# The last stage of a fused attention and spectral-mix kernel: part of an add moved to VectorE and GpSimd, identity matmuls issued earlier, and idle matmuls between the last spectral mixes

## The chip, the cores and the metric

One Trainium2 chip, one of its cores. The metric is the device time in microseconds of one execution of the whole program; a median over several executions is given. Five engines take part, each with its own instruction queue: TensorE (PE; its weight loads are listed as PEld), VectorE (DVE), ScalarE (ACT), GpSimd (POOL) and SyncE (SP). Transfers run on 16 DMA engines; here they are triggered from SP and from POOL.

## The reference

Linear attention over 8 batches, 8 heads, 576 rows and head size 64 gives x with 8 x 576 rows of 512 features. Then, per batch:

```python
X = rfft(x, axis=1)                       # along the 576 rows
Yr = einsum('bmd,mde->bme', Xr, w_r) - einsum('bmd,mde->bme', Xi, w_i)   # first 64 modes only
Yi = einsum('bmd,mde->bme', Xr, w_i) + einsum('bmd,mde->bme', Xi, w_r)
y = irfft(Y, n=576, axis=1)
u = x + y
out = u + maximum(u @ w_ch, 0)
```

The output is 8 x 576 x 512 in fp32, 9.44 MB. The mix weights w_r and w_i hold 64 matrices of 512 x 512 each and are read in fp32.

## The kernel before, in words

Batches are taken in four pairs (`bp`), features in four groups of 128 (`g`). The main loop (L503 to L571) walks 16 units of one group and one pair: feature maps, the attention sums, the forward transform by matmul with a table. In between stand the **mixes** (`mix`, L412 to L453): one takes 8 modes of w_r or w_i for one group, loaded by one DMA of 1 MB from POOL's queue, and adds 16 small matmuls into a PSUM bank, 8 for each call (two calls, `i` = 0 and 1, make one set `o` of 8 modes). Until L572 every engine is held to the written order (`InOrder`, L25); from L573 on a scheduler may reorder what the engines get, within the data's dependences.

After the units come the mixes of the last group. Each second call now ends a set of modes: VectorE adds the earlier groups' sum and stores it as `yst` (L437), SP sends `yst` to `yall` (which lies in the buffer XT, so the profile calls it XT), TensorE transposes `yst` by four identity matmuls, ScalarE copies the result to `yT` (L443), four matmuls multiply it by w_ch, ScalarE copies that to `zst` (L451), and SP sends `zst` to `zall` (L452). `yall` and `zall` thus hold the spectrum of y and of y @ w_ch. Between these mixes run the 36 `channels` calls (L460 to L471), which compute x @ w_ch for one **chunk** of 128 rows and leave it in `xw`. The calls are used up before the last four mix calls, so these have nothing between them.

The **last stage** (L599 to L626) makes the output, chunk by chunk: 36 chunks, nine for each pair, number `n` = 8 being the leftover rows of both batches. For each chunk two PSUM banks are filled: one with x (an identity matmul, L607) plus the inverse transform of `yall` (a matmul with the table CI, L609, or two half-width ones for `n` = 8, L613), the other with x @ w_ch (identity, L607) plus the inverse transform of `zall`. ScalarE takes the relu of the second into `rl` (L618), and VectorE adds the first and `rl` into the output tile `of` or `ofr` (L620). SP stores four chunks at a time, 1 MB (L622), and each pair's leftover in two halves (L626).

The PSUM pool of this stage, `pst`, has eight banks, and it is opened only after the two earlier pools `ps1` (four tiles of one bank) and `ps2` (two tiles of two banks) are closed (L594 to L596). `rl` has two buffers.

Of the kernel before, what the change touches and what calls it, by code (L numbers as in the profile page):

```python
# [10 lines left out]
F32 = mybir.dt.float32  # L11
BF16 = mybir.dt.bfloat16
I32 = mybir.dt.int32
ACT = mybir.ActivationFunctionType
ALU = mybir.AluOpType
# [4 lines left out]
DMODEL = 512  # L20
NG = 4
NP = 4
# [21 lines left out]
def kernel(  # L44
# [13 lines left out]
    nc = tc.nc  # L58
    pe, dve, act = (InOrder(tc, e) for e in (nc.tensor, nc.vector, nc.scalar))
# [9 lines left out]
    def one(shape, dt=F32):  # L69
        return ps1.tile(shape, dt, name="one", tag="one")  # L70

    def two(shape, dt=F32):
        return ps2.tile(shape, dt, name="two", tag="two")
# [6 lines left out]
    XTb = [pers.tile([128, 10, B_, NMODES], BF16, name=f"XT{i}") for i in range(2)]  # L80

    pw_cm = tc.tile_pool(name="pw", bufs=8)
    pw = pw_cm.__enter__()
# [223 lines left out]
    ident_b = const.tile([128, 128], BF16, name="ident_b")  # L307
# [26 lines left out]
    wchb = const.tile([128, 4, 512], BF16, name="wchb")  # L334
    CF = const.tile([128, 6, 4, 64], BF16, name="CF")
    CI = const.tile([128, 5, 128], BF16, name="CI")
# [8 lines left out]
    def sc(i):  # L345
# [4 lines left out]
        out=ang[:, :, 1, :],  # L350
        in0=sf.unsqueeze(2).to_broadcast([128, 5, 64]),
        in1=mf.unsqueeze(1).to_broadcast([128, 5, 64]),
        op=ALU.mult,
# [4 lines left out]
        out=rnd, in0=ang, scalar1=1.0 / S_, scalar2=MAGIC, op0=ALU.mult, op1=ALU.add)  # L358
    dve.tensor_scalar(
        out=rnd, in0=rnd, scalar1=-MAGIC, scalar2=-float(S_), op0=ALU.add, op1=ALU.mult)  # L360
# [48 lines left out]

    pys = {}  # L410

    def mix(g, w, wt, XT):  # L412

        o, i = w // 2, w % 2
        if i == 0:
            pys[o] = one([128, DMODEL])
        py = pys[o]
        for t in range(2):
            s0 = 2 - 2 * t + 4 * i
            for j in range(4):  # L420
                pe.matmul(
                    py[32 * j:32 * j + 32, :],
                    lhsT=XT[:, s0:s0 + 4, :, 32 * t + 4 * o + j].rearrange("p r b -> p (r b)"),
                    rhs=wt[:, 4 * t + j, :], start=(i == t == 0), stop=(i == t == 1),
                )
        if i == 0:
            return
        del pys[o]
        if g == 0:
            act.copy(yacc[:, o, :], py)  # L430
        elif g < NG - 1:
            dve.tensor_tensor(
                out=yacc[:, o, :], in0=py, in1=yacc[:, o, :], op=ALU.add)
        else:

            yst = pb.tile([128, DMODEL], BF16, name="yst")
            dve.tensor_tensor(out=yst, in0=py, in1=yacc[:, o, :], op=ALU.add)  # L437
            sp.dma_start(
                yall[16 * o:16 * o + 16], yst)
            pt = one([128, 4, 128], BF16)  # L440
            for dc in range(4):
                pe.transpose(pt[:, dc, :], yst[:, dc * 128:(dc + 1) * 128], ident_b)
            yT = pb.tile([128, 4, 128], BF16, name="yT")  # L443
            act.copy(yT, pt)
            pz = one([128, DMODEL])
            for dc in range(4):
                pe.matmul(
                    pz, lhsT=yT[:, dc, :], rhs=wchb[:, dc, :],
                    start=(dc == 0), stop=(dc == 3))
            zst = pb.tile([128, DMODEL], BF16, name="zst")  # L450
            act.copy(zst, pz)  # L451
            sp.dma_start(  # L452
                zall[16 * o:16 * o + 16], zst)  # L453

    def chunk(bp, n):
        if n < 8:
            return xs[:, :, bp, 2 * n:2 * n + 2, :].rearrange("p g h d -> p g (h d)")
        return xs[:, :, bp, 16:18, :].rearrange("p g h d -> p g (h d)")

    def channels(bp, n):  # L460
        x = chunk(bp, n)
        pt = one([128, 4, 128], BF16)
        for g in range(NG):
            nc.tensor.transpose(pt[:, g, :], x[:, g, :], ident_b)  # L464
        xT = pb.tile([128, 4, 128], BF16, name="xT")
        nc.vector.tensor_copy(xT, pt)  # L466
        pf = one([128, DMODEL])
        for g in range(NG):
            nc.tensor.matmul(  # L469
                pf, lhsT=xT[:, g, :], rhs=wchb[:, g, :], start=(g == 0), stop=(g == 3))  # L470
        nc.scalar.copy(xw[:, bp, n, :], pf)  # L471


    wts = {}
    wq = [(g, mg) for g in range(NG) for mg in range(2 * NO)]
    mixq = []

    def next_w(n):
        for _ in range(n):
            if wq:  # L480
                key = wq.pop(0)
                wts[key] = wload(*key)

    def some(n):
        for _ in range(n):
            if mixq:
                key = mixq.pop(0)
                mix(*key, wts.pop(key), XTb[key[0] % 2])
                if key == (0, 2):
                    clear(XTb[1])  # L490
                if key not in held:
                    next_w(1)
# [79 lines left out]
    for e in (pe, dve, act, pool, sp):  # L572
# [4 lines left out]
    pb_cm = tc.tile_pool(name="pb", bufs=2)  # L577
    pb = pb_cm.__enter__()
    xw = pb.tile([128, NP, 9, DMODEL], BF16, name="xw", bufs=1)
    zall = pb.tile([128, B_, DMODEL], BF16, name="zall", bufs=1)  # L580
    yall = XTb[0].rearrange("p s b m -> p (s b m)")[:, 0:B_ * DMODEL].rearrange(
        "p (b e) -> p b e", b=B_)
    todo = [(bp, n) for bp in range(NP) for n in range(9)]
    while mixq:
        key = mixq.pop(0)
        if key not in wts:
            next_w(1)
        mix(*key, wts.pop(key), XTb[key[0] % 2])
        next_w(1)
        for _ in range(2):  # L590
            if todo:
                channels(*todo.pop(0))

    ps1_cm.__exit__(None, None, None)  # L594
    ps2_cm.__exit__(None, None, None)
    pst = ctx.enter_context(tc.tile_pool(name="pst", bufs=8, space=bass.MemoryType.PSUM))  # L596


    for bp in range(NP):  # L599
        of = [pw.tile([128, 4, DMODEL], F32, name="of", tag="wt") for _ in range(2)]  # L600
        ofr = pb.tile([128, DMODEL], F32, name="ofr")
        for n in range(9):
            ps = []
            for base, src in ((chunk(bp, n), yall), (xw[:, bp, n, :], zall)):
                p = pst.tile([128, DMODEL], F32, name="pt", tag="pt")
                po = p.rearrange("p (g e) -> p g e", g=4) if src is yall else p
                nc.tensor.matmul(po, lhsT=ident_b, rhs=base, start=True, stop=False)  # L607
                if n < 8:
                    nc.tensor.matmul(p, lhsT=CI[:, n % 4, :], rhs=src[:, 2 * bp + n // 4, :],  # L609
                                     start=False, stop=True)  # L610
                else:
                    for i in range(2):
                        nc.tensor.matmul(  # L613
                            p[64 * i:64 * i + 64, :], lhsT=CI[:, 4, 0:64],
                            rhs=src[:, 2 * bp + i, :], start=False, stop=True)
                ps.append(p)
            rl = pb.tile([128, DMODEL], F32, name="rl")
            nc.scalar.activation(rl, ps[1], ACT.Relu)  # L618
            o = of[n // 4][:, n % 4, :] if n < 8 else ofr
            nc.vector.tensor_tensor(out=o, in0=ps[0], in1=rl, op=ALU.add)  # L620
            if n in (3, 7):
                nc.sync.dma_start(  # L622
                    out[2 * bp + n // 4, 0:512, :].rearrange("(p c) e -> p c e", c=4),
                    of[n // 4])
        for i in range(2):
            nc.sync.dma_start(out[2 * bp + i, 512:576, :], ofr[64 * i:64 * i + 64, :])  # L626
    pb_cm.__exit__(None, None, None)
    pw_cm.__exit__(None, None, None)

# [1 line left out]
_INS = ['q', 'k', 'v', 'w_phi', 'moe_w_r', 'moe_w_i', 'moe_w_ch']  # L631
# [26 lines left out]
```

The softmax here doesn't subtract the row's maximum and nothing guards it: scores larger than these inputs give would overflow.

## Time and profile before

| what | value |
|---|---|
| median of 7 executions | 482.41 us (480.55 to 482.71) |
| the profiled execution, its own time | 480.75 us |
| its span on the core | 478.9 us |
| TensorE matmul busy | 326.8 us (68%) |
| VectorE busy | 288.8 us (60%) |
| ScalarE busy | 256.4 us (54%) |
| GpSimd busy | 104.0 us (22%) |
| bytes written to HBM | 9.44 MB |
| mean granted TensorE clock | 0.882 |

The profiled execution lies 1.7 us below the median. Its span starts and ends with the core's work; the 1.8 us between span and time lie around it. In the rows below, a time without another word is in us from the start of the span. The profile page gives busy time by engine, the span cut into 40 slices, the chain of work that ended last, and groups of instructions with the mean time of one. The trace can also be asked for instructions in order of time, for busy time and granted clock in chosen stretches, and for all instructions that touch one tile.

### The profile page before, as it was taken

The page shows a single profiled execution, that of the slowest core. Times are in us where ns is not written, and L with a number is a line of the kernel's source. Part 1 is how long each engine was busy: PE and PEld are TensorE (multiplying, and loading weights), DVE is VectorE, ACT ScalarE, POOL GpSimd, SP SyncE. Part 2 cuts the span into 40 slices and gives each one's busy share as a digit, 9 for nine tenths or more (in the row PEclk, how much of TensorE's full clock was granted, in tenths as well). Part 3 has the DMA queues.
Part 4 walks back from the last instruction along what each step waited for, and adds up shares of the span by engine and source line. Part 5 has one row for each costly group of instructions (what it writes and reads, how often), then busy time and mean ns, then how long its engine had stood idle before and what let it go on. Part 6 is the DMA issues. An engine that isn't in the chain of part 4 may idle for free. (4 is left out here: it accounts for less than half of the span.)

```text
span 478.9 us, 8054 instructions
## 1 busy us (share of the span) xinstructions
PE 326.8 (68%) x3104; PEld 202.7 (42%) x3133; DVE 288.8 (60%) x524; ACT 256.4 (54%) x435; POOL 104.0 (22%) x139
## 2 busy tenths in 40 slices
PE   2563776787767876786587646747667676737994
PEld 1352554555544544554465334523333333312441
DVE  5678579779779778878869657632221222200874
ACT  3761767767776965865675727401232333301763
POOL 8332122124412331322043121131211110000000
PEclk9999977759999988977978859777999999985998
DMA  8999999999999999999999999999999999990676
GB/s 140 212 213 208 212 207 212 215 212 204 217 210 210 212 217 205 214 216 205 215 218 203 219 204 207 207 208 208 206 207 215 216 215 214 214 192 25 242 296 252
DMA packets 111318, 99.68 MB, mean 208 GB/s; under 512 B 16944, under 2 KB 109744, under 8 KB 110256
## 3 DMA queue, kind: packets, MB, share of 16 engines
q0 software_dynamic: 84496, 76.03, 97.5%
q1 hardware_dynamic: 26784, 23.14, 18.5%
q8 instruction: 24, 0.39, 0.3%
q14 instruction: 14, 0.11, 0.1%
HBM read 163.64 MB, written 9.44 MB: 361 GB/s over the span
## 5 line engine op out<-in xcount | busy, mean ns | idle before, releaser
L37 ACT ACTIVATE AB<-two 128x1024 bf16<-128x1024 f32 x64 | 62.0, 1021 | 46.8 <-DVE mk L37 46.4
L37 ACT ACTIVATE AQ<-two 128x1024 bf16<-128x1024 f32 x64 | 62.7, 1043 | 16.3 <-PE two L37 11.8
L471 ACT CAST xw<-one 128x512 bf16<-128x512 f32 x36 | 21.1, 585 | 67.6 <-PE one L469 60.3
L37 DVE TENSOR_TENSOR nd<-one,e 128x390 f32<-128x390 f32 x48 | 26.8, 558 | 49.6 <-PE one L37 49.5
L37 PE MATMUL one<-wt,XT 128*32 128x512 bf16 x472 | 38.5, 429 | 23.9 <-DMA wt<-in_moe_w_i_dram 19.1
L466 DVE COPY xT<-one 128x512 bf16<-128x512 bf16 x36 | 15.3, 424 | 62.6 <-PE one L464 62.6
L37 POOL DMA_DIRECT2D wt<-in_moe_w_r_dram x29 | 25.6, 884 | 110.6 <-PE one L37 70.4
L469 PE MATMUL one<-wchb,xT 128*128 128x512 bf16 x135 | 38.1, 396 | 14.6 <-DVE xT L466 14.0
L37 PE MATMUL one<-va,AB 128*128 128x65 bf16 x512 | 30.6, 221 | 21.2 <-DVE va L37 21.1
L37 DVE TENSOR_TENSOR va<-vn,ee 128x1152 bf16<-128x1152 f32 x32 | 41.9, 1352 | 0.0
L37 DVE TENSOR_REDUCE mk<-two 128x8 f32<-128x1024 f32 x32 | 39.0, 1218 | 4.1 <-PE two L37 4.0
L37 PE MATMUL one<-kvz,AQ 128*128 128x65 bf16 x512 | 30.7, 207 | 14.8 <-ACT kvz L37 10.4
L37 DVE TENSOR_REDUCE mq<-two 128x8 f32<-128x1024 f32 x32 | 37.6, 1215 | 1.1 <-PE two L37 1.1
L37 PEld LDWEIGHTS <-AB 128*128 128x128 bf16 x512 | 25.5, 116 | 27.9 <-issue 13.5
L37 POOL DMA_DIRECT2D wt<-in_moe_w_i_dram x30 | 26.4, 881 | 49.1 <-PE one L37 23.6
L37 PEld LDWEIGHTS <-XT 128*32 128x32 bf16 x512 | 21.4, 167 | 36.7 <-issue 29.7
L37 PEld LDWEIGHTS <-AQ 128*128 128x128 bf16 x512 | 26.4, 107 | 24.7 <-issue 21.3
L37 POOL DMA_DIRECT2D qb<-in_q_dram x32 | 22.9, 721 | 56.4 <-DVE nd L37 34.7
L37 POOL DMA_DIRECT2D kb<-in_k_dram x32 | 22.9, 719 | 54.3 <-PE one L37 18.1
L37 PE MATMUL one<-CF,xs 128*128 128x256 bf16 x160 | 30.3, 358 | 2.2 <-DVE xs L37 2.2
L37 PE MATMUL one<-ident_b,kb 128*128 128x128 bf16 x144 | 15.2, 250 | 24.3 <-DMA kb<-in_k_dram 15.0
L37 DVE TENSOR_TENSOR nd<-one,nd 128x390 f32<-128x390 f32 x48 | 27.1, 565 | 5.8 <-PE two L37 0.5
(91 smaller groups left out, 589.7 us busy)
## 6 DMA issues: line engine op xcount, KB each, us to landing
wt<-in_moe_w_i_dram POOLq DMA_DIRECT2D x30, 1024.0 KB, 27.1
wt<-in_moe_w_r_dram POOLq DMA_DIRECT2D x29, 1024.0 KB, 26.6
vn<-in_v_dram SPq DMA_DIRECT2D x32, 256.0 KB, 8.0
out_dram<-of SPq DMA_DIRECT2D x8, 1024.0 KB, 3.9
kb<-in_k_dram POOLq DMA_DIRECT2D x32, 128.0 KB, 20.7
qb<-in_q_dram POOLq DMA_DIRECT2D x32, 128.0 KB, 16.8
kf<-in_k_dram SPq DMA_DIRECT2D x32, 32.0 KB, 6.0
vn<-in_v_dram SPq DMA_DIRECT2D x32, 32.0 KB, 6.5
```

The lines of the kernel that those rows point to most:

```text
L37: ins = f(*args, **kwargs)
L466: nc.vector.tensor_copy(xT, pt)
L469: nc.tensor.matmul(pf, lhsT=xT[:, g, :], rhs=wchb[:, g, :], start=(g == 0), stop=(g == 3))
L471: nc.scalar.copy(xw[:, bp, n, :], pf)
```

## The change

In the last stage, for every second chunk from the sixth on (`late`: place 5, 7, ..., 35 in the new order, 16 of 36), the identity matmul that brings x into the first bank is left out. VectorE adds x while it reads the bank, without the relu, and GpSimd then adds the relu `rl` onto the result in SBUF. For the other 20 chunks all stays as it was. The pair's leftover chunk (`n` = 8) now comes first of its nine. `rl` gets three buffers. The last stage uses the pools `ps1` and `ps2` on, in place of a new pool, with the banks of a chunk taken from a two-bank tile or from two one-bank tiles in turn.

The identity matmuls of the first two chunks are issued before the last mix call, those of the third behind it. TensorE is again held to the written order from the fourth-last mix call on. Into a spare bank `idle`, matmuls with no use for their result are issued: 14 and 8 after the fourth-last and third-last call, 8 after the second-last, and, in each of the two calls that end a set, 3 ahead of the transposes and 3 behind them. The leftover tile `ofr` holds all four pairs, and the last four chunks are stored one at a time (256 KB each).

```diff
-    def mix(g, w, wt, XT):
+    def mix(g, w, wt, XT, warm=None):
...
             sp.dma_start(
                 yall[16 * o:16 * o + 16], yst)
+            if warm:
+                warm(3)
             pt = one([128, 4, 128], BF16)
             for dc in range(4):
                 pe.transpose(pt[:, dc, :], yst[:, dc * 128:(dc + 1) * 128], ident_b)
+            if warm:
+                warm(3)
...
+    order = [(bp, n) for bp in range(NP) for n in (8, 0, 1, 2, 3, 4, 5, 6, 7)]
+    sums = {}
+    def late(idx):
+        return idx >= 4 and idx % 2 == 1
+    def start(idx):
+        bp, n = order[idx]
+        if idx < 2 or idx % 3 == 0:
+            t = two([128, 2, DMODEL])
+            u, w = t[:, 0], t[:, 1]
+        else:
+            u, w = one([128, DMODEL]), one([128, DMODEL])
+        if not late(idx):
+            pe.matmul(u.rearrange("p (g e) -> p g e", g=4), lhsT=ident_b, rhs=chunk(bp, n),
+                      start=True, stop=False)
+        pe.matmul(w, lhsT=ident_b, rhs=xw[:, bp, n, :], start=True, stop=False)
+        sums[idx] = u, w
+    def warm(n):
+        for _ in range(n):
+            pe.matmul(idle, lhsT=ident_b, rhs=wchb[:, 0, :], start=True, stop=True)
     while mixq:
...
+        if len(mixq) == 3:
+            pe.on = True
+            idle = one([128, DMODEL])
-        mix(*key, wts.pop(key), XTb[key[0] % 2])
+        mix(*key, wts.pop(key), XTb[key[0] % 2], warm if len(mixq) < 4 else None)
+        if len(mixq) == 1:
+            start(0)
+            start(1)
+            warm(8)
+        elif len(mixq) in (2, 3):
+            warm(14 if len(mixq) == 3 else 8)
...
+    for idx, (bp, n) in enumerate(order):
+        if idx == 0:
+            start(2)
...
+        if idx not in sums:
+            start(idx)
+        u, w = sums.pop(idx)
+        for p, src in ((u, yall), (w, zall)):
+            first = late(idx) and src is yall
+            if n < 8:
+                pe.matmul(p, lhsT=CI[:, n % 4, :], rhs=src[:, 2 * bp + n // 4, :],
+                          start=first, stop=True)
...
+        rl = pb.tile([128, DMODEL], F32, name="rl", bufs=3)
+        nc.scalar.activation(rl, w, ACT.Relu)
+        if late(idx):
+            og = o.rearrange("p (g e) -> p g e", g=4)
+            nc.vector.tensor_tensor(
+                out=og, in0=u.rearrange("p (g e) -> p g e", g=4), in1=chunk(bp, n), op=ALU.add)
+            nc.gpsimd.tensor_tensor(out=o, in0=o, in1=rl, op=ALU.add)
+        else:
+            nc.vector.tensor_tensor(out=o, in0=u, in1=rl, op=ALU.add)
...
+            c0, c1 = (0, n % 4 + 1) if n % 4 == 3 else (0, 0)
+            if bp == NP - 1 and n >= 4:
+                c0, c1 = n % 4, n % 4 + 1
```

## The prediction

> **What bounds the kernel now.** I read the page's slices first, then the chain that ended last, then the timeline of the last 47 us engine by engine.
>
> ```profile
> PE   2563776787767876786587646747667676737994
> DVE  5678579779779778878869657632221222200874
> PEclk9999977759999988977978859777999999985998
> DMA  8999999999999999999999999999999999990676
> ```
>
> ```profile
> DMA wt<-in_moe_w_i_dram 9%; PE pt L607 4%; PE pt L609 3%; PE one L37 1%; PE pt L613 1%; PE one L469 0%; ACT rl L618 0%; DVE xT L466 0%; DVE yst L37 0%; DVE ofr L620 0%; ACT zst L37 0%; ACT yT L37 0%; PE one L464 0%; POOL wt L37 0%; ACTq L37 0%
> ```
>
> The DMA row is full up to slice 36: until the last mix weights land, the transfers set the pace. Behind that the chain is a short serial stretch (one L37) and then the last stage, PE L607, L609, L613. The change touches only what follows 418 us, so all of its effect lies here:
>
> ```profile
> 432.08 1.09 PE L37 MATMUL one<-wt,XT 128*32 128x512 bf16 x8 [4.86 <-DMA wt<-in_moe_w_i_dram]
> 433.97 0.61 PE L37 MATMUL one<-ident_b,yst 128*128 128x128 bf16 x4 [0.80 <-DVE yst L37]
> 435.31 1.89 PE L37 MATMUL one<-wchb,yT 128*128 128x512 bf16 x4 [0.73 <-ACT yT L37]
> 437.92 0.58 PE L607 MATMUL pt<-xs,ident_b 128*128 128x512 bf16 x1 [0.72 <-ACT zst L37]
> 438.29 0.63 PE L607 MATMUL pt<-xw,ident_b 128*128 128x512 bf16 x1
> ...
> 443.05 0.38 PE L607 MATMUL pt<-xs,ident_b 128*128 128x512 bf16 x1
> 443.27 0.38 PE L609 MATMUL pt<-XT,CI 128*128 128x512 bf16 x1
> ```
>
> The matmuls of 438 start 0.43 us apart, those of 443 0.216 us apart: half and full granted clock. From 443.05 to 472.67 TensorE never rests (32 chunks: 0.86 us for four matmuls, 1.31 for a leftover chunk), so six chunks take 5.5 us on average. The others keep pace:
>
> ```profile
> 451.59 0.60 ACT L618 ACTIVATE rl<-pt 128x512 f32<-128x512 f32 x1 [0.27 <-PE pt L609]
> 452.22 0.69 DVE L620 TENSOR_TENSOR of<-pt,rl 128x512 f32<-128x512 f32 x1 [0.17 <-ACT rl L618]
> ```
>
> ScalarE waits for TensorE, VectorE for ScalarE, each only a little: VectorE is 0.69 us busy in 0.86. GpSimd does nothing after 389 us, so its adds have nothing ahead of them in its queue.
>
> **The head: load to `zall`.** `zst` is done at 437.86, is sent at 437.89, and the shortest way of such a transfer is 3.1 us (`zall`, issue to landing): 441.0. At full clock the eight mix matmuls take 0.69 (row at 421.68), the transposes 0.39, the four multiplications 1.04 (rows near 412): 0.40 + 0.22 + 0.85 = 1.47 us saved. The idle matmuls, 3 x 0.216 = 0.65 us, lie in the waits of 0.80 and 0.73 above. So `zst` goes off at 436.4 and `zall` lands at 439.5. If the clock is half all the same, three take 1.3 us, overrun both waits by 0.48 and 0.55, and `zall` lands at 442.0. Does the clock stay up? The windows:
>
> ```profile
> 420.37:423.78 3.41, 1.08 (x12) 0.47 (x11) 0.69 (x1) 0.13 (x1) 0.00 (x0) 1.00 1.24 208
> 423.78:427.19 3.41, 2.68 (x11) 0.87 (x13) 0.00 (x0) 1.04 (x2) 0.00 (x0) 0.50 1.23 210
> 430.61:434.02 3.41, 1.14 (x9) 0.28 (x9) 0.69 (x1) 0.00 (x0) 0.00 (x0) 0.50 0.07 18
> 437.44:440.85 3.41, 2.94 (x7) 0.99 (x7) 0.00 (x0) 0.42 (x1) 0.00 (x0) 0.50 0.16 41
> ```
>
> Columns: stretch, its length, busy us of PE, PEld, DVE, ACT, POOL, granted clock, DMA share, GB/s. The clock changed at 423.8, 427.2, 430.6 and 440.85, always a multiple of 3.41 us apart, and by how busy the stretch before was: 1.08 us of PE brought the half, 2.68 and 2.94 the full clock. With 36 idle matmuls between 418.9 and the last load, and six behind it, every such stretch up to 436 is 1.6 us busy or more (least in 430.61 to 434.02: 0.69 for the mix, 0.65 idle matmuls, the transposes), so I take the saving of 1.47. But behind `zst` the new order has only chunk 2's two identity matmuls; TensorE then rests from 436.0 to 439.5. If a stretch ends between about 438.2 and 440.4 (2.2 of 3.41 us, two cases in three) it is nearly empty, and TensorE runs at half clock until 3.41 us later, losing half of the 2 to 4.5 us: 1.3 on average. Two thirds of that is **0.9 us**; bounds 0 and 2.2.
>
> The Trainium skill, "TensorE: Matmul & The Clock Gate", Part 1, says this window of 3.413 us runs free and is not reset by a kernel's start. That speaks against fixed numbers of idle matmuls, which can suit one phase and miss another; by it alone the term would be 0 in one execution and 2.2 in the next. No single trace shows that.
>
> **The last stage: what goes.** 16 identity matmuls of 0.216 us, 3.5 us of TensorE. The first eight identities (437.92 to 441.07, at half clock) were beside `zall`'s transfer; now six are ahead and the others behind. So TensorE alone would be some 4 to 5 us earlier. DVE's work stays 36 x 0.69: an add with x in place of `rl`, the same shape, out of PSUM; taken at 0.69 (bounds: 0.60, the `va` product's 1.35 us for 1152 elements scaled to 512, and 0.75 if x's four pieces cost a little; the range holds both). The leftover chunk moved to the front, one `ofr` tile and three more stores on SP (0.34 to 0.55 us each, an idle queue) I cost at nothing; ScalarE's 36 x 0.60 stays.
>
> **What comes: GpSimd's add of two fp32 128x512 tiles.** No such row exists. The nearest:
>
> ```profile
> masks.py:199 POOL TENSOR_SCALAR_AFFINE_SELECT ident_f<-ident_f 128x128 f32<-128x128 f32 x1 | 0.3, 292 | 0.1
> masks.py:197 POOL MEMSET ident_f<- 128x128 f32 x1 | 0.2, 204 | 0.3 <-POOLq L642 0.3
> L642 POOL MEMSET const-float32-0.0<- 128x1 f32 x1 | 0.1, 98 | 0.2 <-issue 0.2
> ```
>
> A start of about 98 ns; (204 - 98)/127 = 0.83 ns per element written, (292 - 98)/127 = 1.53 read and written. A second read at the same 0.70 makes 2.23, so 0.10 + 511 x 0.00223 = **1.24 us**, my value. Ends: 0.69, VectorE's row, and 1.76, two affine passes of 0.88.
>
> "GPSIMD Engine Reference", § 3, calls GpSimd the wrong choice for ordinary elementwise work and gives 4497 ns for this add at 2048 elements. A quarter is 1.12 us as an estimate from that page; by it the sum below is 1.7 lower, 482.2.
>
> **Who waits for it.** `rl` is held until GpSimd has read it, and there are three. In the built program's waits, the relu of chunk 7 waits for GpSimd's add of 5, that of 9 for 7, that of 13 for 11, that of 15 for 13, and so on every six chunks; VectorE's add of 9 (15, 21, ...) waits for that chunk's relu. Behind a waiting relu stand all later ones on ScalarE, and PSUM banks come free only three chunks on, so TensorE stops too. The ring from relu 7's end to relu 13's: add 7, relu 9, VectorE's add 9, add 9, add 11, relu 13 = 3 x 1.24 + 0.60 + 0.69 + 0.60 + six hand-overs of about 0.05 = **5.9 us for six chunks**. TensorE needs 3 x 0.86 + 3 x 0.65 = 4.5; before it was 5.5.
>
> **The sum.** `zall` 439.5. Chunks 0 to 2 follow; chunk 3's first identity needs chunk 0's bank, freed after relu and add, 441.3; 11 matmuls bring 443.7, relu 5 ends 444.5, add 5 445.8, relu 7 446.45. Four rings of 5.93: relu 31 at 470.2. Then add 31, relu 33, VectorE 33, adds 33 and 35 with hand-overs: 475.5. The last store needs 3.1 us to land and 0.9 to the span's end (before, the last packet ended at 477.3, 1.6 before the span's end: landing and closing together): 479.5. The store queue says the same: 1 MB issued after add 31 (471.5), then four pieces, at 0.36 MB/us (before, the last 1.31 MB took 473.7 to 477.3). With the clock's 0.9: 480.4 against 478.9, so +1.5. On the profiled execution that is 482.2; on the median, 1.7 higher, **483.9**. The sum moves 14 us for each us of GpSimd's add: the last two are covered by the store queue.
>
> **Rivals.** (1) *GpSimd is quicker.* At 0.88 (one-input price) the ring takes 4.9, near TensorE's own need; 14 x 0.36 = 5.0 less: 478.9, faster. For it: the affine row does more arithmetic than an add. Against it: one read fewer. It decides from 1.06 us down (14 x 0.18 = 2.5 less than the forecast). (2) *The idle matmuls don't hold the clock*: `zall` at 442.0 and not 439.5, 486.4. For it: the stretch 430.61 to 434.02 gets only 0.43 + 0.65 us of streaming. (3) *No change*: an add of 1.06 to 1.20 us just gives back what TensorE saves, 481.4 to 483.4. (4) *GpSimd at 1.4 or more*, sharing SBUF with VectorE: 14 x 0.16 and up, 486.1 and more.
>
> **Numbers.** Forecast (an add of 1.20 to 1.40) 0.38; (1) 0.28; (2) 0.08; (3) 0.20; (4) 0.06. Slower by over 0.2% 0.52 (forecast, 2, 4), within 0.2% (about what a measurement of this kernel can tell from no change) 0.20, faster 0.28. Range 479.0 to 487.0: down to rival 1, up to rival 2 and a GpSimd add of 1.46; the forecast's own is 483.3 to 486.1.
>
> **What would show it.** GpSimd's adds at 1.1 to 1.35 us; ScalarE's idle time in the last stage ended by POOL; TensorE with gaps; VectorE under 0.69 in 0.95; `zall` issued near 436.4; half clock somewhere after 438. I am wrong if ScalarE waits for TensorE as before, or if GpSimd's add is under 1.05.

## The result, and the profile after

The changed kernel takes **484.94 us** (median of 20 executions, 482.48 to 486.12), the kernel before 482.33 us (47 executions, 480.55 to 483.89): ratio 1.0057, 95% interval 1.0047 to 1.0067. It is slower by 2.6 us; the forecast of 483.9 us was 1.0 us short. The profiled execution took 484.45 us, with a span of 482.7.

The slices and the chain of the changed kernel, in the page's form (the second line of the chain lists engine and source line; helpers share L37, L653 is the relu, L656 and L660 VectorE's adds, L658 GpSimd's):

```profile
PE   2563776778887966876686555847667675796983
POOL 8332222123312422331133121222111110000564
PEclk9999979777878887988989859758899998998998
DMA  8999999999999999999999999999999999981676
PE one L37 3%; POOL of L658 2%; DVE of L656 1%; PE two L37 1%; ACT rl L653 1%; DMA zall<-zst 1%; PE one L473 0%; POOLq L701 0%; POOL ofr L658 0%; ACT yT L37 0%; DVE xT L470 0%; DVE yst L37 0%; DVE of L660 0%; ACT zst L37 0%; PE one L468 0%
```

Before, GpSimd's row was empty at the end:

```profile
POOL 8332122124412331322043121131211110000000
```

Now GpSimd is busy in the last three slices, 0.4 to 0.6 of them, and stands second in the chain. TensorE's last four digits, 7994, have become 6983: it rests while others work.

**The head**, the instructions of TensorE in order of time (start, duration, engine, line, what; in brackets the idle time before and what ended it):

```profile
433.44 0.69 PE L37 MATMUL one<-wt,XT 128*32 128x512 bf16 x8
...
434.92 0.40 PE L37 MATMUL one<-ident_b,yst 128*128 128x128 bf16 x4
...
436.05 1.04 PE L37 MATMUL one<-wchb,yT 128*128 128x512 bf16 x4
...
441.77 0.64 PE L37 MATMUL two<-zall,CI 128*64 128x512 bf16 x2 [3.49 <-DMA zall<-zst]
```

The 8 mix matmuls, the transposes and the four multiplications have their full-clock durations (0.69, 0.40, 1.04), with three idle matmuls in each of the gaps left out. `zall` is triggered at 437.78, 4.34 us after the last mix starts; before it was 5.81. Then TensorE rests for 3.49 us. The windows from that rest on (stretch, its length, busy us of PE, PEld, DVE, ACT, POOL with counts, granted clock, DMA share, GB/s):

```profile
437.70:441.12 3.42, 0.41 (x2) 0.18 (x2) 0.00 (x0) 0.06 (x1) 0.00 (x0) 1.00 0.19 45
441.12:444.53 3.41, 2.76 (x8) 0.94 (x8) 1.17 (x2) 1.45 (x3) 0.00 (x0) 0.50 0.00 1
444.53:447.94 3.41, 3.36 (x16) 1.54 (x16) 2.85 (x5) 2.35 (x5) 0.40 (x1) 1.00 0.36 79
```

The empty window 437.70 to 441.12 is followed by one at half clock, in which the first chunks are made.

**The last stage.** What ScalarE waited for from 430 us on (us in total, times, longest), and its relus in order of time:

```profile
ACT rl L653 <- POOL of L658: 9.8, 12, 1.1
...
ACT rl L653 <- POOL ofr L658: 2.2, 2, 1.1
```

```profile
454.75 1.09 ACT L653 ACTIVATE rl<-one 128x512 f32<-128x512 f32 x2 [0.64 <-POOL of L658]
456.72 0.60 ACT L653 ACTIVATE rl<-two 128x512 f32<-128x512 f32 x1 [0.89 <-POOL of L658]
...
459.42 0.60 ACT L653 ACTIVATE rl<-two 128x512 f32<-128x512 f32 x1 [1.12 <-POOL of L658]
460.65 1.09 ACT L653 ACTIVATE rl<-one 128x512 f32<-128x512 f32 x2 [0.64 <-POOL of L658]
```

Before, ScalarE's idle time in this stage was ended by TensorE, but for 0.8 us in 3 waits:

```profile
ACT rl L618 <- PE pt L609: 11.2, 25, 4.5
...
ACT rl L618 <- PE pt L613: 2.1, 4, 0.6
...
ACT rl L618 <- DVE of L620: 0.8, 3, 0.3
```

Now GpSimd ends 12.0 us of it, in 14 waits. Chunks are numbered from 0 in the order in which the last stage makes them. The pattern repeats every six chunks: relu 13 starts at 454.75, relu 19 at 460.65, relu 25 at 466.56, relu 31 at 472.46, so 5.90 us for six. The price of one add (group of instructions: count, busy us, mean ns, idle before):

```profile
L658 POOL TENSOR_TENSOR of<-of,rl 128x512 f32<-128x512 f32 x14 | 17.6, 1268 | 65.4 <-ACT rl L653 60.4 <-DVE of L656 4.3 <-DVE of L660 0.7
```

And one period of the ring, from the rows of three engines, read downwards as "who had to end for the next":

```profile
461.33 1.27 POOL L658 TENSOR_TENSOR of<-of,rl 128x512 f32<-128x512 f32 x1 [0.71 <-ACT rl L653]
...
462.63 0.60 ACT L653 ACTIVATE rl<-two 128x512 f32<-128x512 f32 x1 [0.89 <-POOL of L658]
...
463.26 0.69 DVE L656 TENSOR_TENSOR of<-two,xs 128x512 f32<-128x512 f32 x1 [0.79 <-ACT rl L653]
...
464.03 2.49 POOL L658 TENSOR_TENSOR of<-of,rl 128x512 f32<-128x512 f32 x2 [1.43 <-DVE of L656]
...
466.56 1.09 ACT L653 ACTIVATE rl<-one 128x512 f32<-128x512 f32 x2 [0.63 <-POOL of L658]
```

GpSimd's add of chunk 19 ends, and relu 21 may start. VectorE's add of 21 runs behind it, then GpSimd's adds of 21 and 23, and then relu 25. Each row begins within 0.1 us of the end of the one above. From 448.13 us on, TensorE has no place in the chain that ended last.

One member of this ring is not asked for by the data: VectorE's late add (L656) reads x and the first bank, not `rl`. Yet it waits for its chunk's relu wherever the chunk's two banks are halves of one two-bank tile (`two`: chunks 9, 15, 21, 27 and 33, the two leftover chunks among them), and never where they are two tiles:

```profile
L656 DVE TENSOR_TENSOR of<-one,xs 128x512 f32<-128x512 f32 x11 | 7.5, 682 | 0.2 <-PE one L37 0.2
...
L656 DVE TENSOR_TENSOR of<-two,xs 128x512 f32<-128x512 f32 x3 | 2.1, 691 | 2.4 <-ACT rl L653 2.4
...
L656 DVE TENSOR_TENSOR ofr<-two,xs 128x512 f32<-128x512 f32 x2 | 1.4, 690 | 1.6 <-ACT rl L653 1.6
```

Without this wait GpSimd's add of 21 could start at relu 21's end, 463.23, and not at 464.03: by these rows up to 0.8 us less for six chunks, an estimate. No run takes the wait away.

### The profile page after: what moved, and what is told of

The parts are those of the page before. It is cut to its first block, busy times and chain, and to the rows that moved or that the text cites. A ratio compares the mean times of both kernels' runs of the same rounds, so it can differ in the third digit from the quotient of the medians.

```text
span 482.7 us, 8142 instructions
## 1 busy us (share of the span) xinstructions
PE 333.0 (69%) x3129; PEld 203.7 (42%) x3159; DVE 287.6 (60%) x524; ACT 255.0 (53%) x435; POOL 124.0 (26%) x155
## 5 line engine op out<-in xcount | busy, mean ns | idle before, releaser
L37 ACT ACTIVATE AB<-two 128x1024 bf16<-128x1024 f32 x64 | 62.0, 1021 | 48.4 <-DVE mk L37 48.1
L37 ACT ACTIVATE AQ<-two 128x1024 bf16<-128x1024 f32 x64 | 62.6, 1042 | 15.4 <-PE two L37 11.7
L37 DVE TENSOR_TENSOR nd<-one,e 128x390 f32<-128x390 f32 x48 | 26.8, 558 | 50.1 <-PE one L37 50.1
L37 POOL DMA_DIRECT2D wt<-in_moe_w_r_dram x29 | 25.6, 881 | 112.5 <-PE one L37 83.6
L37 PE MATMUL one<-wt,XT 128*32 128x512 bf16 x472 | 40.8, 451 | 15.2 <-DMA wt<-in_moe_w_i_dram 11.2
L37 PE MATMUL one<-va,AB 128*128 128x65 bf16 x512 | 31.6, 226 | 22.2 <-DVE va L37 22.1
L37 PE MATMUL one<-kvz,AQ 128*128 128x65 bf16 x512 | 30.2, 205 | 18.3 <-ACT kvz L37 12.8
L37 DVE TENSOR_TENSOR va<-vn,ee 128x1152 bf16<-128x1152 f32 x32 | 41.9, 1352 | 0.0
L37 DVE TENSOR_REDUCE mk<-two 128x8 f32<-128x1024 f32 x32 | 39.0, 1218 | 3.7 <-PE two L37 3.6
L37 POOL DMA_DIRECT2D wt<-in_moe_w_i_dram x30 | 26.4, 879 | 48.5 <-PE one L37 30.7
L37 PEld LDWEIGHTS <-AB 128*128 128x128 bf16 x512 | 26.6, 119 | 28.5 <-DVE va L37 14.3
L37 POOL DMA_DIRECT2D qb<-in_q_dram x32 | 22.9, 719 | 60.4 <-PE one L37 24.1
L37 DVE TENSOR_REDUCE mq<-two 128x8 f32<-128x1024 f32 x32 | 37.6, 1215 | 1.1 <-PE two L37 1.1
L37 PEld LDWEIGHTS <-AQ 128*128 128x128 bf16 x512 | 25.8, 106 | 29.1 <-issue 26.0
L37 POOL DMA_DIRECT2D kb<-in_k_dram x32 | 22.9, 719 | 50.5 <-DMA wt<-in_moe_w_i_dram 16.6
L658 POOL TENSOR_TENSOR of<-of,rl 128x512 f32<-128x512 f32 x14 | 17.6, 1268 | 65.4 <-ACT rl L653 60.4
L37 PEld LDWEIGHTS <-XT 128*32 128x32 bf16 x512 | 21.0, 169 | 29.1 <-issue 22.9
L37 DVE TENSOR_TENSOR nd<-one,nd 128x390 f32<-128x390 f32 x48 | 27.1, 565 | 5.7 <-PE two L37 0.5
L37 PE MATMUL one<-ident_b,kb 128*128 128x128 bf16 x144 | 14.3, 244 | 22.6 <-DMA kb<-in_k_dram 20.1
```

The source lines that it names most:

```text
L37: ins = f(*args, **kwargs)
L658: nc.gpsimd.tensor_tensor(out=o, in0=o, in1=rl, op=ALU.add)
```

## The experiments

The theory after the result has two parts: (a) the three `rl` buffers, shared by chunks that GpSimd ends and chunks that VectorE ends, make a ring of waits that sets the pace; (b) the rest ahead of `zall` costs half clock behind it. Rivals: GpSimd's adds themselves, or contention with VectorE, are the bound whatever the buffers; the head's saving didn't come; the idle matmuls delay the last mix; the stores set the end. Since executions differ by 1 to 2 us in when the last weights land, the table also gives the time from the start of the last mix to the span's end, in which that part of the scatter is absent.

The ratio is to the kernel before, measured beside each (482.03 to 482.33 us). The last three columns are us of the one profiled execution.

| kernel | median us | ratio to before, 95% interval | last mix to end (profiled) | trigger of `zall` to its first matmul | from there to the fifth relu |
|---|---|---|---|---|---|
| before | 482.33 | 1 | 46.8 | (no wait) | |
| changed | 484.94 | 1.0057, 1.0047 to 1.0067 | 49.3 | 3.99 | 4.44 |
| e1 own buffers (2+2) | 479.37 | 0.9954, 0.9934 to 0.9974 | 43.6 | 3.13 | 4.78 |
| e2 no late chunks | 481.56 | 0.9990, 0.9981 to 1.0000 | 46.2 | 3.40 | 4.94 |
| e3 half the add | 478.75 | 0.9932, 0.9915 to 0.9949 | 44.0 | 4.14 | 4.83 |
| e5 no idle matmuls | 485.68 | 1.0064, 1.0045 to 1.0083 | 50.3 | 3.14 | 4.83 |
| e6 e1 with fewer idle | 480.39 | 0.9951, 0.9936 to 0.9967 | 45.5 | 3.88 | 5.91 |
| e7 e1 with the rest filled | 477.72 | 0.9898, 0.9878 to 0.9918 | 42.5 | 3.12 | 3.74 |
| e8 e6 with the rest filled | 478.89 | 0.9921, 0.9902 to 0.9939 | 43.6 | 4.19 | 3.74 |
| e9 own buffers (2+1) | 481.27 | 0.9976, 0.9961 to 0.9991 | 46.6 | 4.15 | |
| e10 two shared | 487.91 | 1.0113, 1.0089 to 1.0136 | 54.5 | 4.08 | |
| e11 rest filled alone | 482.30 | 0.9999, 0.9986 to 1.0012 | 47.7 | 3.11 | 3.74 |
| e12 e7 again | 477.65 | 0.9894, 0.9874 to 0.9914 | 42.5 | 3.11 | 3.74 |

### Whose buffers: e1, e9, e10

e1 gives the late chunks' relus two buffers of their own and the others two:

```diff
-        rl = pb.tile([128, DMODEL], F32, name="rl", bufs=3)
+        rl = pb.tile([128, DMODEL], F32, name="rg" if late(idx) else "rl", bufs=2)
```

> The change with one edit: the relu of a late chunk goes into buffers of its own (two), that of the other chunks into two others, four in all and not three shared ones. GpSimd does the same 16 adds. Theory (the ring of waits on rl sets the last stage): relu 9 now waits for GpSimd's add of 5 and not of 7, the ring of 5.9 us for six chunks is gone, TensorE's 4.5 to 4.8 us for six sets the pace, and the time falls by 5 to 6 us, to 479 to 480 us, below the kernel before; ScalarE no longer waits for POOL. Rival A (GpSimd's rate, or its sharing of SBUF with VectorE, is the bound): nothing falls, 484 to 486. Rival B (the loss lies in the half clock and in the later weights, not in the last stage's pace): at most 1 us less.

Measured: 479.37 us, 5.6 us less than the changed kernel and less than the kernel before. ScalarE's waits of e1 from 430 us on, and the chain that ended last, over part of the stretch shown above:

```profile
ACT rl L653 <- PE two L37: 6.2, 8, 3.7
ACT rl L653 <- PE one L37: 2.8, 12, 0.3
ACT rg L653 <- PE two L37: 0.5, 2, 0.2
```

```profile
461.16 1.51 PE one L37 x7
462.67 0.77 PE two L37 x5
463.44 1.62 PE one L37 x7
```

No wait for GpSimd is left, and the chain is TensorE without a gap, although GpSimd's adds are as long as before (1270 ns). So its speed was not the bound: 16 adds of 1.27 us are 20 us of a stage of about 30.

e9, two and one, three in all:

```diff
+        rl = pb.tile([128, DMODEL], F32, name="rg" if late(idx) else "rl", bufs=2 if late(idx) else 1)
```

> Three relu buffers in all, as in the changed kernel, but two of them for the late chunks (read by GpSimd) and one for the others (read by VectorE). Theory: it is not the number of buffers but that GpSimd's and VectorE's relus take turns on the same three, so that VectorE's add of chunk 9 waits, through relu 9, for GpSimd's add of 7. With buffers of their own the waits of relu for GpSimd go away; the others' single buffer makes a ring of its own, relu 0.60 + VectorE's add 0.69 + two hand-overs and a little waiting for VectorE's queue, about 1.6 us for two chunks, 4.8 to 5.1 for six: between TensorE's 4.5 and the 5.5 of the kernel before. I expect 3 us less than the changed kernel: 481.5 to 482.3, ratio to before 0.998 to 1.000. Rival: three buffers are too few however they are shared out: 484.5 to 485.5, ratio 1.005 or more.

Measured: 481.27 us, 3.7 less than the changed kernel with the same three buffers. ScalarE waited for VectorE (7.3 us in 13 waits) and never for GpSimd; the pattern of six chunks takes 4.8 us (relus of the same kind at 453.95, 458.65, 463.56, 468.26 and 473.00). So the sharing alone explains 3.7 of the 5.6 us that e1 gained. The number counts as well: e1, with a buffer more, is 1.9 us below e9. Four buffers shared by all were not run.

e10, two shared by all:

```diff
+        rl = pb.tile([128, DMODEL], F32, name="rl", bufs=2)
```

> The changed kernel with two shared relu buffers in place of three. Theory (the ring is buffers held by GpSimd): each relu then waits for the add two chunks before, for late chunks GpSimd's at 1.27 us; with an even number the late chunks always get the same buffer: relu 0.60 and GpSimd's add 1.27, with VectorE's add 0.69 now behind every wait in ScalarE's queue, about 2.1 us for two chunks, 6.4 for six against 5.91: 4 us slower than the changed kernel, 488 to 490, ratio 1.012 to 1.016. Rival: the pace is GpSimd's or the stores' own, not that of the buffers: 485 to 486.

Measured: 487.91 us, 3.0 more than the changed kernel; a little under the expected 488 to 490. The relus of e10, one period and a bit:

```profile
462.64 0.60 ACT L653 ACTIVATE rl<-one 128x512 f32<-128x512 f32 x1 [1.61 <-POOL of L658]
...
469.29 0.60 ACT L653 ACTIVATE rl<-one 128x512 f32<-128x512 f32 x1 [1.61 <-POOL of L658]
```

Six chunks take 6.65 us (462.64 to 469.29) against 5.90: over four rings 3.0 us, as much as the difference of the medians. This profiled execution itself took 490.62 us, 2.7 above the median of its six; from last mix to end it is 5.2 us longer than the changed kernel's, and the four rings are 3.6 of that (relu 7's end at 451.31, relu 31's at 478.52).

### GpSimd's price, and no GpSimd: e3, e2

e3 halves the add, and so leaves the relu out of half of the columns of the late chunks:

```diff
+            nc.gpsimd.tensor_tensor(out=o[:, 0:256], in0=o[:, 0:256], in1=rl[:, 0:256], op=ALU.add)
```

> The change with GpSimd's add cut to 256 of the 512 columns; the relu of the other 256 columns of the 16 late chunks is left out of the output. All waits are the same. GpSimd's add should take about 0.1 + 255 x 0.0023 = 0.68 us and not 1.27. Theory: 14 of the 16 adds lie on the ring, so up to 14 x 0.59 = 8 us go, until TensorE's own pace stops it: the ring is 3 x 0.68 + 2.2 = 4.2 us, under TensorE's 4.5, so 5 to 6 us less, 479 to 480. Rival A (sharing of SBUF, not length): GpSimd's instructions still take over 1 us. Rival B: at most 1 us less.

Measured: 478.75 us, 6.2 less than the changed kernel, with three shared buffers. The half add:

```profile
L658 POOL TENSOR_TENSOR of<-of,rl 128x256 f32<-128x256 f32 x14 | 10.2, 725 | 66.3 <-ACT rl L653 61.6 <-DVE of L656 4.5
```

256 columns less save 543 ns, 2.12 ns per element, and (725 - 543) leaves a start of about 0.18 us, by a straight line through the two lengths. ScalarE waited for TensorE again. At the prediction's 14 us for each us of add it would have been 7.6 less; TensorE took over before that.

e2 keeps all identities on TensorE, and VectorE adds the relu everywhere:

```diff
-        return idx >= 4 and idx % 2 == 1
+        return False
```

> The change without its late chunks: all 36 have the identity matmul and VectorE's add with the relu, GpSimd adds nothing; order, early identities and idle matmuls stay. Theory: the last stage is TensorE-bound again at about 5.5 us for six chunks, the head keeps its 1.5 us, the half clock after zall takes back 0.9 on average; the time is 481 to 482, 3 to 3.5 us under the change and 0.5 to 1.5 us under the kernel before. Rival B (the loss lies in the head: early identities, idle matmuls, half clock): 484 or more, slower than before though GpSimd does nothing.

Measured: 481.56 us, 0.5 less than the kernel before beside it (482.03): that is what the new head, pools and stores are worth together, the half clock behind the rest included. So the late chunks with shared buffers cost 3.4 us (484.94 - 481.56), and with buffers of their own they gain 2.2 (481.56 - 479.37).

e4 is the kernel before, unchanged:

> The kernel before, unchanged, for a second profile. Question: are the 1.4 us by which the last weights landed later with the change (433.4 against 432.1 us) the change's doing? If executions differ by themselves, this one's last weights land somewhere between 432 and 434.5 us and its time follows; if not, at 432.1 again.

The kernel before once more took 481.19 us in its only execution, with the last mix at 432.11 (432.08 in the profile shown), the trigger of `zall` 5.80 us behind and 47.3 us from the last mix to the end. In the twelve profiles of changed programs the last mix starts between 432.8 and 434.3; but both profiles of before lie over 1 us below their median, so no step of the change is made answerable for that, and none is cleared of it.

### The idle matmuls: e5, e6

In e5 `warm` issues nothing:

```diff
-        for _ in range(n):
+        for _ in range(0):
```

> The changed kernel with every idle matmul taken out (the early identities, the shared rl and GpSimd's adds stay). Theory: the idle matmuls hold the clock from the last load to zst, which saved 1.47 us (4.34 us from load to trigger of zall, against 5.81 before), but they also stand in TensorE's queue ahead of the last mix: in the changed kernel this mix started 0.4 to 0.7 us later after the issue of its weights (44.3 to 44.6 us) than in the kernel before (43.8 to 43.9), with no wait for the load. Without them I expect the mix to wait for its load again, 43.8 us after the issue, and 5.8 us from there to the trigger: 49.6 against 48.7 us, so 0.9 us slower than the changed kernel, 485.4 to 486.0, ratio to before about 1.007. Rival: the clock stays up without them, or their hold is worth no more than they delay: 484.3 to 485.0, ratio 1.005 or less.

Measured: 485.68 us, 0.7 more than the changed kernel, though the intervals overlap. The last mix to the trigger takes 5.80 us again, so the saving of 1.46 there is the idle matmuls' doing. In its profile the trigger comes 1.46 us later than in the changed kernel, the landing 0.85 sooner after it, the fifth relu 0.39 later after that: 1.0 in all, as 50.3 against 49.3 in the table. The other half of the theory, that they delay the last mix, is tried by e6, which is e1 with fewer of them:

```diff
-            warm(14 if len(mixq) == 3 else 8)
+            warm(8)
```

> The version with separate buffers for the late and the other relus, and 8 in place of 14 idle matmuls after the fourth-last mix call. Theory: the idle matmuls make the last mix late by 0.4 to 0.7 us; with 6 x 0.217 = 1.3 us fewer it waits for its load again (idle time of 0.5 to 0.9 us ended by DMA wt), 43.8 us after the issue in place of 44.5, and the clock stays full: about 0.5 us less than the version with separate buffers alone, 478.9, ratio to before about 0.9945. Rival: the load itself lands that late, or the stores set the end: no change, 479.4, ratio 0.9955.

Measured: 480.39 us, 1.0 more than e1 where 0.5 less was expected, though the ratio is as e1's. Here the last mix waits 1.42 us for its load, and still starts 44.6 us after that load's issue, as late as in the kernels where it stands right behind idle matmuls (44.3 to 44.6). The load takes 42.7 to 45.0 us in the kernels that wait for it, so its own scatter hides the effect in the times. The landings in the traces show a small one. Where the mix waits for its load, it starts 0.04 to 0.05 us after the landing; in the four profiles where idle matmuls stand right ahead of it, it starts 0.14 to 0.54 us after it (433.27 to 433.44 in the changed kernel, 432.23 to 432.77 in e2). In the five other profiles with the same 14 idle matmuls the load came later than they ended.

### The rest ahead of `zall`: e11, e7, e8, e12

One line more, in e11 alone, in e7 and e12 on top of e1, in e8 on top of e6 (the expectations stand in the order e11, e7, e8, e12):

```diff
             start(2)
+            warm(12)
```

> The changed kernel (three shared buffers) with 12 more idle matmuls behind the third chunk's identities and nothing else. It prices the prediction's term of 0.9 us (bounds 0 and 2.2) for the empty stretch ahead of zall. Theory: the first chunks are made at full clock in every execution, so the ring starts 0.9 to 1.6 us earlier: 483.4 to 484.0, ratio 1.0023 to 1.0038, and the times of single executions lie closer together. Rival: behind a ring of 5.91 us TensorE's clock does not count: 484.9, ratio 1.0055.

> The version with separate buffers, and 12 more idle matmuls after the identities of the third chunk, so that TensorE does not rest while zall is on its way. Theory (the term of 0.9 in the prediction): the empty stretch ahead of zall brings half clock for 3.41 us in which the first chunks are made; filled, the clock is full from the last load on, and about 13 matmuls start 0.216 in place of 0.43 us apart: 0.9 to 1.5 us less than with separate buffers alone, 478.0 to 478.5, ratio 0.992 to 0.9935. Rival: the stores set the end now (the last add ends 4.9 us ahead of the span's end, and the DMA engines are 0.84 to 0.97 busy in the last 15 us), so earlier chunks gain little: 479.0 to 479.5.

> All three: separate buffers, 8 in place of 14 idle matmuls, 12 more while zall is on its way. If both theories hold, the gains add up: 0.5 + 1.2 below separate buffers alone, 477.7, ratio about 0.991. If the stores set the end, 479, ratio 0.994 or more.

> The best version so far once more (separate buffers, 12 more idle matmuls while zall is on its way). Theory: 477.7 again, ratio 0.989 to 0.991; the landing of zall, 3.1 to 4.2 us after its trigger, and that of the last weights move single executions by 1 to 2 us. Rival: the first measurement was lucky, and it is nearer to the version with fewer idle matmuls: ratio 0.992.

Measured: 482.30, 477.72, 478.89 and 477.65 us: each 1.5 to 2.6 us less than its partner without the filling, more than expected for e11 and e7; e8 fell 1.2 short of its 477.7. The window of the first chunks in e7, filled, and three windows of e6, not filled:

```profile
440.83:444.24 3.41, 2.97 (x14) 1.27 (x13) 2.34 (x4) 2.44 (x5) 0.00 (x0) 1.00 0.25 56
```

```profile
438.07:441.48 3.41, 0.57 (x3) 0.28 (x3) 0.00 (x0) 0.40 (x1) 0.00 (x0) 1.00 0.18 44
441.48:444.90 3.42, 2.52 (x7) 0.86 (x7) 0.94 (x2) 1.21 (x3) 0.00 (x0) 0.50 0.01 1
444.90:448.31 3.41, 3.41 (x9) 1.21 (x8) 1.83 (x3) 1.19 (x3) 0.00 (x0) 0.50 0.35 77
```

All eight profiles without the filling show half clock behind the first `zall` matmul, e6 and e10 for two windows in a row; the four with it show none. From the first `zall` matmul to the fifth relu it is 3.74 us in every filled one, and 4.44 to 5.91 in the six others that have the same first chunks, so the half clock costs 0.70 to 2.17 us, 1.2 on average. e11 gained 2.6 at the median (0.0058 of the time, give or take 0.0016). Part of the remaining 1.4 may be the landing of `zall`, 3.1 to 4.2 us after its trigger in filled and unfilled kernels alike (3.1 in three of the four filled ones); that is not settled.

e7 and e12 are the version that is fastest, 1.0 to 1.1% below the kernel before. There the stores come near the end, though they did not swallow the gain: GpSimd's last add ends at 470.53 in e7 and the span at 475.4, 4.9 us later, against 4.4 in the changed kernel.

## Why the prediction was right, step by step

The sum for the profiled execution started at a last mix of 432.08 and gave a span of 480.4, so 48.3 us. Measured from its own last mix (433.44) it is 49.3. In the order of the steps:

| step | predicted | measured |
|---|---|---|
| last mix to trigger of `zall` | 4.3 | 4.34 |
| trigger to the first `zall` matmul | 3.1 | 3.99 |
| from there to relu 7's end | 6.95, and 0.9 for the clock | 7.67, with the clock |
| four rings, to relu 31's end | 23.7 | 23.6 |
| relu 31 to the last add's end | 5.3 | 5.25 |
| last add to the span's end | 4.0 | 4.4 |

- **The head: right.** 1.47 us saved; the idle matmuls lie in the waits and the clock is full up to 441.12. Rival 2 is out.
- **The landing of `zall`: 0.9 short.** 3.1 us was the shortest way, taken as the price. The twelve profiles of changed programs show 3.1 to 4.2, 3.6 on average. The mean was the value to take.
- **The clock behind the rest: right in kind, low in size.** Taken at two cases in three and 0.9 us; it came in all eight unfilled profiles, and cost 1.2 us on average in the six that can be compared. The term was also low by its own numbers: half of 2 to 4.5 us is 1.0 to 2.25, 1.6 in the middle and not 1.3. In e11, without it, first `zall` matmul to relu 7's end took 6.97 us, the 6.95 of the sum. The bound of 2.2 counted one window; two in a row occur, when the first chunks at half clock leave gaps (2.52 us busy in e6's window kept the half, 2.76 in the changed kernel's brought the full clock).
- **GpSimd's add: 1.24 taken, 1.27 measured.** From two rows of other instructions; e3 gives the same build in its own numbers, a start of 0.18 and 2.12 ns per element (taken: 0.10 and 2.23). That it came within 0.03 us is partly luck: the start was too low and the slope too high, and the working rested on the guess that a second read costs as much as the first, with 48 chances in 100 given to the rivals (1) and (3) of a quicker add. Rivals 1 and 3 needed 1.20 or less, and 4 needed 1.4.
- **The ring: right.** Its terms add up to 5.91 us (the sum used 5.93), 5.90 measured. Its members, in the predicted order, are the rows shown above; e10 lengthens it, e1, e3 and e9 break it. TensorE's own need was put at 4.5 us for six chunks; in e1, where TensorE sets the pace, it is 4.7 (relu 7's end at 448.38, relu 31's at 467.26).
- **VectorE's add with x: 0.69 taken, 0.68 to 0.69 measured** (L656).
- **"TensorE alone would be some 4 to 5 us earlier": in line.** With ring and rest gone, e12 lies 4.6 us below the kernel before (482.22 beside it).
- **Sum.** +0.9 (landing) - 0.2 (clock, this execution) - 0.1 (rings) + 0.4 (end) = +1.0 us. The forecast at the median lacked 1.0 us too, but only because two more errors nearly cancel: in the profiled execution the last mix started 1.4 us later than in the one before, and the median lies 0.5 us above the profiled execution, where 1.7 had been added.

"TensorE: Matmul & The Clock Gate", Part 1 of the Trainium skill, says that the clock's window runs free of the kernel's start. The profiles agree: in the eight unfilled kernels the half clock starts anywhere between 440.15 and 442.99 us. By that rule alone, as the prediction read it, the clock's term could be 0 in some executions; none of the eight shows that.

"GPSIMD Engine Reference", § 3, gives 4497 ns for this add at 2048 elements. The start and slope of e3 and the changed kernel give 0.18 + 2048 x 0.00212 = 4.52 us, in agreement; the quarter of it, 1.12, was 0.14 us short of the measured 1.27, about three quarters of that start: the start doesn't shrink with the size.

## What to carry to other kernels

Before work goes to a slower engine, ask which buffers it holds and who else needs them next: here the same three buffers with owners of their own were worth 3.7 us, and four with owners 5.6, and with them the moved work itself was no burden (2.2 us gained over e2). Where results of two engines take turns in one pool, write the ring down (who frees, who waits, who stands behind the waiter) and compare its period with the bottleneck's. A rest of some microseconds on TensorE costs again behind it, in half-clock work; price it by its mean over the phases, and price a transfer by its mean, not by its best.

## What the runs showed of the hardware, unexpected

- GpSimd and VectorE hardly slowed each other: GpSimd's adds took 1268 ns in the changed kernel and 1270 in e1, where VectorE worked closer together, and 1255 to 1262 for the last two of the changed kernel, the second of them after VectorE's last add (476.95). VectorE's stayed at 0.68 to 0.69 us.
- VectorE's adds of 0.69 us start 0.60 us apart when nothing holds them (452.06, 452.65 and 453.25 in the changed kernel): the spans of neighbours overlap by 0.09.
- The same 128 KB transfer of `zall` lands 3.1 us after its trigger in one execution and 4.2 in another, with the DMA engines nearly empty in both (0.18 busy from 438 to 441 us in e11, 0.20 in e8).
